# A delta-rule attention and an MLP on one core: work of the opening stage put in another order over ScalarE and VectorE

## The chip, the core and the metric

The kernel runs on one NeuronCore of a Trainium2 chip. The metric is the device time of one execution in microseconds (us); the time of a kernel is the median of its runs. The engines are TensorE (PE: matmuls and transposes, into PSUM), VectorE (DVE), ScalarE (ACT), GpSimd (POOL) and SyncE (SP, which issues nearly all loads). Each engine works off its own instructions in their order; a wait at the head of a queue holds everything behind it. Unless said otherwise, a time such as "at 43.6 us" is counted from the start of the profiled span.

## The reference

Two blocks run one after the other. The first is a delta-rule attention over 4 batches, 8 heads, 768 steps and head size 48; the second is an MLP over the 3072 rows of the first's output.

```python
k_n = k / (np.linalg.norm(k, axis=-1, keepdims=True) + 1e-06)
for t in range(S):                       # S = 768, state is (B, H, 48, 48)
    y[:, :, t] = einsum('bhd,bhde->bhe', q[:, :, t], state)
    v_old = einsum('bhde,bhd->bhe', state, k_n[:, :, t])
    state += b_t * einsum('bhd,bhe->bhde', k_n[:, :, t], v[:, :, t] - v_old)
x = y.transpose(0, 2, 1, 3).reshape(3072, 384)
h = x @ w_in                             # 384 x 2048
out = (0.5 * h * (1 + erf(h / sqrt(2)))) @ w_out      # 2048 x 384
```

The weights `w_in` and `w_out` come as 64-bit floats, which the kernel turns into 32-bit floats itself.

## The kernel before

**Tiles.** Time is cut into 12 chunks of 64 steps (`NC`). A chunk has two units (`NA`), each with two batches and 8 heads: 128 partitions are 2 batches x 64 steps. `tiles[c, a]` is unit `a` of chunk `c`; `first` are the four units of chunks 0 and 1, `zero` those of chunk 0, `one` of chunk 1, `third` of chunk 2, `fourth` of chunk 3. A unit's tiles are `Kp`, `Qp`, `V` (loaded), `Kt`, `Qt` (transposed), `P` (masked scores), `W`, `U` and `x`.

**A chunk's attention.** The recurrence within a chunk is a triangular system. Two chunks are a group, solved together: `grams` multiplies K with K, `flip` puts the 32 x 32 diagonal blocks into `Nu`, and 30 row steps on VectorE (`row_product`, L490, and `row_sum`, L495) invert them one row after another. `back` transposes the result into `XM` (L504) and `Zf` (L508). `join` (chunk pair 0, L529) or `join_run` (later pairs, L571) builds the off-diagonal block in two levels: TensorE's `psJ`, VectorE's product into `XM` (L540 or L583), `psJ` again, ScalarE's copy into `Zf` (L544 or L552). Then `against_state` (`psK`, L645), `subtract` (ScalarE copies `y`, L657, VectorE makes `W`, L658 and L659), `solve` (`psU`, L675, then copies to `U`, L680 and L682), `use` (`psY`, L694 and L703), `next_state` (L708), `read` (`x` out of `psY`, L716 for chunks 0 and 1, L718 later) and `turn` (transposes `psX`, then the copy to `xT`, L740).

For these a K row's length is needed. For chunks 2 and 3 `sum_of_squares` (L317, ScalarE, one head at a time) adds up squares, `prep` takes roots on GpSimd (`pow`, L332), `finish_both` makes the factors (L288 to L292), and `scale_head` (L355, ScalarE, one head at a time) multiplies V by the length; `scale_v` does so on GpSimd from chunk 4 on.

**The MLP.** For chunk `c`, `fc1(c, f)` makes hidden block `f` of 16 (six matmul records in `psH`, L763) and ScalarE's gelu writes it to `G` (L765). `psH` and `psO` share two PSUM buffers, so block `f` starts when the gelu of block `f - 2` is through. For chunks 0 and 1 `fc2` multiplies by `w_out` (`psO`, L776), with the copy to `o_sb` (L780) and two output DMAs issued by ScalarE (L770). From chunk 2 on the second product goes by Strassen's scheme with seven products (`second_layer`, L801, and VectorE's sums, L810 to L858); its weight sums need tiles that `late` makes room for, once the weights are decoded. `late` also makes the two `Kb` tiles, which must be cleared (L1007, ScalarE) before chunk 5's keys are loaded into them in blocks.

**The weights.** They come in 16 groups: 0 to 7 of `w_in` (two hidden blocks each), 8 to 15 of `w_out` (two `f` each). A group is decoded in five steps on VectorE, with one on ScalarE: `start_` (exponent bits, L218, then ScalarE's L223 into `w_e`), `upper` (L227), `lower` (L232), `sign` (L240, which needs L223) and `scaled` (L244, after which TensorE may use the group). Steps of group n + 1 stand between those of group n.

**What sets the order.** Up to the turn of chunk 0 all engines follow the order in which the code is written (`by_hand`, L907). After that a plan gives each step a due time: `on(first, last, steps)` spreads steps between two times on a scale where 57 to 115 is one chunk, `once` puts steps at one time, `at` counts in chunks. The steps are sorted by it; up to and including `late`, VectorE and ScalarE keep exactly that order, after it VectorE alone, and the scheduler orders the rest. `together` keeps the matmuls of its steps in one run on TensorE. Due times give an order, not a moment. `rows1` is the list of elimination steps of pair 1; `alternate(group(10, NW - 1), rows1[2:42])` mixes the decoding of the last groups with 40 of its row steps.

In the opening, ScalarE copies each `Qt` and `P` of chunks 0 and 1, and between units does four squares of chunk 2's K and four scalings of chunk 1's V:

```python
        queries([u])
        for h in range(4 * u.t, 4 * u.t + 4):
            sum_of_squares(tiles[2, h // H], h % H)
        for h in range(4 * u.t, 4 * u.t + 4):
            scale_head(tiles[1, h // H], h % H)
```

Of the kernel before, what the change touches and what calls it, by code (L numbers as in the profile page):

```python
# [16 lines left out]
def kernel(  # L17
# [28 lines left out]
    nc = tc.nc  # L46
    B, H, S, D = q.shape
# [91 lines left out]
    def load_v(c):  # L139
        if c >= NC:  # L140
            return
        for a in range(NA):
            u = tiles[c, a]
            u.V = io.tile([128, H, D], F32, tag="V", name="V", bufs=4)
            fetch_in(u.V, v, u)
# [162 lines left out]
    def sum_of_squares(u, h):  # L308

        if "both" not in ns:  # L310
            n23 = wk.tile([128, 2 * NA, H], F32, tag="n23", name="n23", bufs=1)
            ns[2], ns[3] = n23[:, 0:NA], n23[:, NA:]
            ns["both"] = n23
        if h == 0:
            u.ksq = wk.tile([128, H, D], F32, tag="ksq", name="ksq")
        kn = u.Kn if u.c == 2 else Qp[2 + u.a]
        nc.scalar.activation(u.ksq[:, h], kn[:, h, 0:D], ACT.Square,  # L317
                             accum_out=ns[u.c][:, u.a, h:h + 1])
# [593 lines left out]
    for n in range(2):  # L912
        fetch(n)
    load_k(2, "Kp")
    load_v(1)
    new_group(0)
    n0 = wk.tile([128, 2 * NA, H], F32, tag="n0", name="n0", bufs=1)
    for c in range(2):
# [21 lines left out]
    for u, ahead in zip(first, first[1:] + [None]):  # L940
        if ahead is not None:
            transposed(ahead, (1,))
        queries([u])
        for h in range(4 * u.t, 4 * u.t + 4):
            sum_of_squares(tiles[2, h // H], h % H)
        for h in range(4 * u.t, 4 * u.t + 4):
            scale_head(tiles[1, h // H], h % H)
    for a in range(NA):
        fetch_in(tiles[2, a].Qp[:, :, 0:D], q, tiles[2, a])
    for a in range(NA):  # L950
        fetch_in(Qp[2 + a][:, :, 0:D], k, tiles[3, a])
    for n in range(2, NS):
        fetch(n)
    for n in range(n_in, n_in + len(slots)):
        fetch(n)
    third = [tiles[2, a] for a in range(NA)]
# [22 lines left out]
    for step in (begin, exponents, upper, lower):  # L979
        for n in range(2):  # L980
            step(n)
    solve(first[:NA])
    sign(0)
    sign(1)
    use(first[:NA])
    for u in first[:NA]:
        read(u)
    scaled(0)
    scaled(1)
    for u in first[:NA]:  # L990
# [10 lines left out]
    def late():  # L1001
        start.close()
        more.append(ctx.enter_context(tc.tile_pool(name="late", bufs=1)))
        small[0] = ctx.enter_context(tc.tile_pool(name="few", bufs=1, space=bass.MemoryType.PSUM))
        for a in range(NA):
            Kb = more[0].tile([128, 2, NP, 2, HB], F32, name=f"Kb{a}")
            nc.scalar.mul(Kb.rearrange("q p j h n -> q (p j h n)"),  # L1007
                          low.rearrange("q a b -> q (a b)")[:, 0:NP * 4 * HB], 0.0)
            for c in range(5, NC, 2):
                tiles[c, a].Kb = Kb  # L1010

    def on(first, last, steps):

# [10 lines left out]
    def group(n, last=None):  # L1024
# [8 lines left out]
             once(79.2, (together, (solve, one))), once(83.2, (together, (use, one))),  # L1033
             once(85.2, *[(read, u) for u in one]), once(87.6, *[(next_state, u) for u in one]),
             once(87.7, *[(turn, u) for u in one])]
    plan += [on(57.8, 72.0, [(1.0, sum_of_squares, tiles[3, a], h)
                             for a in range(NA) for h in range(H)]),
             once(73.0, (load, 3), (prep, 2), (prep, 3))]
    plan += [on(54.3, 57.9, group(2)), on(57.9, 61.4, group(3)), on(61.4, 65.0, group(4)),
             on(67.5, 71.0, group(5)), on(71.0, 74.6, group(6)), on(76.8, 80.4, group(7)),  # L1040
             on(80.4, 84.0, group(8)), on(84.0, 87.5, group(9)),
             once(87.8, (finish_both,), *[s_[1:] for s_ in rows1[:2]]),
             on(91.9, 126.0, alternate(group(10, NW - 1), rows1[2:42])),
             on(126.1, 128.4, rows1[42:-3]), once(128.6, (late,))]
    for i in range(NF // 2):
        t = (84.2, 88.3)[i] if i < 2 else 92.1 + 5.68 * (i - 1)
        plan += [on(t, t + 2.5, [(1.0, fc2, u, 2 * i, 2 * i + 2) for u in zero])]
# [1 line left out]
        if i < EARLY // 2:  # L1049
# [6 lines left out]
    s2 = state_steps(2)  # L1056
    plan += [once(128.5, *[s_[1:] for s_ in rows1[-3:-1]]),
             once(131.6, (together, (against_state, third))), once(131.7, (subtract, third)),
             once(133.0, (together, join1[0])), once(133.1, rows1[-1][1:]),
             once(136.0, (together, join1[1]), (copy_out, "join", 4)),  # L1060
             once(138.0, (queries, third)), once(139.0, s2[1][1:]),
             once(140.0, (together, join1[2]), (copy_out, "join", 4)),
             once(143.0, s2[2][1:]), once(147.0, s2[3][1:], s2[4][1:]),
             once(141.0, (prep, 4)), once(150.0, (grams, [tiles[4, a] for a in range(NA)])),
             once(160.0, (finish, 4))]
    plan += [at(0.995, 1.0, [(1.0, load_v, 2)]), at(2.98, 2.981, [(1.0, sums_of_w)]), at(3.1, 3.11, [(1.0, last_sum_of_w)])]
    plan += [at(c - 0.4, c - 0.3, v_steps(c)) for c in range(4, NC)]
    plan += [at(c - 1.0, c - 0.99, [(1.0, load_v, c)]) for c in range(3, NC)]
    for c in range(4, NC):
        us = [tiles[c, a] for a in range(NA)]  # L1070
        t = {4: 1.8, 5: 2.25}.get(c, c - 2.9)
        plan += [at(t, t + 0.01, [(1.0, load_blocks, c, "Kb", k)])]
        t = 3.2 if c == 4 else c - (1.3 if c % 2 == 0 else 0.9)
        plan += [at(t, t + 0.01, [(1.0, load_blocks, c, "Qb", q)])]
        t = c - (2.1 if c % 2 == 0 else 2.4) if c > 5 else {4: 2.1, 5: 2.48}[c]
        plan += [at(t, t + 0.01, [(1.0, load_k, c, "Kn")])]
        plan += [at(c - 0.4, c - 0.39, [(1.0, load_k, c, "Kp")])]
        t = {4: 2.47, 5: 2.955}.get(c, c - (1.97 if c % 2 == 0 else 2.49))
        plan += [at(t, t + 0.01, [(1.0, turned_k, u) for u in us])]
        t = c + (0.05 if c % 2 == 0 else -0.34)  # L1080
        plan += [at(t, t + 0.01, [(1.0, turned_q, u) for u in us])]
# [9 lines left out]
    for w in range(3, NC):  # L1091
        two_ahead = w + 2 < NC
        if w % 2:
            if w == 3:
                plan += [at(w + 0.09, w + 0.092, [(1.0, transposed, u, (1,)) for u in fourth]
                            + [(1.0, together, *gram(5))])]
            plan += [at(w + 0.25, w + 0.95, state_steps(w, (), query(w)))]
            if two_ahead:
                rows = eliminate_steps(w // 2 + 1)
                plan += [at(w - (0.05 if w == 3 else 0.16), w - (0.04 if w == 3 else 0.15), [(1.0, prep, w + 2)]),  # L1100
                         at(w, w + 0.01, [(1.0, finish, w + 2)]),
                         at(w + 0.13, w + 0.18, rows[:2]), at(w + 0.18, w + 0.36, rows[2:26]),
                         at(w + 0.4, w + 1.06, rows[26:-3]), at(w + 1.07, w + 1.2, rows[-3:])]
        else:
            j0, j1, j2 = join_steps(w // 2)
            plan += [at(w + 0.23, w + 0.232, [(1.0, together, j0, *query(w))]),
                     at(w + 0.3, w + 0.301, [(1.0, together, j1, *gram(w + 2))]),
                     at(w + 0.35, w + 0.97, state_steps(w, (j2,), gram(w + 3)))]
            plan += spread("join", 2, w + 0.32, w + 0.355)
            plan += spread("join", 4, w + 0.455)  # L1110
            if two_ahead:
                plan += spread("gram", 1, w + 0.385, w + 0.42, w + 0.54, w + 0.58)
                plan += spread("gram", 1, w + 0.66, w + 0.661, w + 0.7, w + 0.701)
                plan += [at(w + 0.59, w + 0.591, [(1.0, prep, w + 2)]),
                         at(w + 0.9, w + 0.91, [(1.0, finish, w + 2)])]
# [36 lines left out]
```

## Time and profile before

| | |
|---|---|
| median of 5 runs | 662.63 us (660.55 to 662.95) |
| the profiled execution | 662.95 us, span 661.2 us |
| granted TensorE clock | 1.00 of full |
| TensorE busy | 633.7 us (96%) |
| VectorE busy | 441.2 us (67%) |
| ScalarE busy | 227.0 us (34%) |
| GpSimd busy | 78.6 us (12%) |
| first `psH` | at 59.3 us |

The page gives each engine's busy time, then the span in 40 slices of 16.5 us whose digits are busy tenths, then the chain of work that ended last, groups of instructions and DMA issues. In a row of the timeline the first number is the start, the second the time from the start of its first to the end of its last instruction, `x4` the number of instructions merged, and the bracket the idle time of that engine before it with what ended it. A row of waits gives the total, the number and the longest. Matmuls are counted in records, two for each f32 matmul of the code.

### The profile page before, as it was taken

What the parts mean: (1) busy time and instruction counts of PE and PEld (TensorE: products, weight loads), DVE (VectorE), ACT (ScalarE), POOL (GpSimd) and SP (SyncE); (2) the same over time, 40 slices, a digit from 0 to 9 for tenths busy, and PEclk for the clock granted to TensorE, in tenths of its full rate; (3) what the DMA queues carried; (4) which work ended last, traced back from release to release, by engine and by line L of the source; (5) the groups of instructions that cost most, each with busy time, mean ns of one, the idle gap of its engine ahead of it and who ended that gap; (6) DMA issues with size and microseconds to landing.
All of it is one profiled execution on the core that took longest, in us unless ns stands there. A gap on an engine that the chain in (4) does not pass through costs nothing.

```text
span 661.2 us, 20444 instructions
## 1 busy us (share of the span) xinstructions
PE 633.7 (96%) x8902; PEld 557.3 (84%) x8902; DVE 441.2 (67%) x920; ACT 227.0 (34%) x616; POOL 78.6 (12%) x79
## 2 busy tenths in 40 slices
PE   6678999899999999999999999999999999999997
PEld 5567887566789889989989989989989989989997
DVE  6969899995399855679755678755678744324022
ACT  3577754335441136132136132135132133131220
POOL 4050020003111011301011301011301010000000
PEclk9999999999999999999999999999999999999999
DMA  9875465033434233520233520212300210100101
GB/s 132 177 257 160 107 152 154 8 60 61 72 44 81 37 41 54 93 42 16 53 40 53 98 39 19 47 19 39 61 15 19 51 17 3 25 2 2 24 1 25
DMA packets 158426, 39.68 MB, mean 60 GB/s; under 512 B 150016, under 2 KB 153216, under 8 KB 158336
## 3 DMA queue, kind: packets, MB, share of 16 engines
q1 hardware_dynamic: 152464, 33.40, 26.5%
q10 hardware_dynamic: 5872, 4.97, 3.5%
q8 instruction: 70, 1.15, 0.8%
q14 instruction: 20, 0.16, 0.1%
HBM read 33.62 MB, written 4.72 MB: 58 GB/s over the span
## 4 chain that ended last, share of the span: by engine, by line
PE 77%; DVE 11%; ACT 3%; SPq 3%; DMA 3%; issue 1%; ACTq 1%; POOL 0%; DVEq 0%; POOLq 0%
PE psH L763 33%; PE psY L801 12%; PE psX L801 11%; PE psZ L801 4%; PE psG L395 3%; PE psK L645 3%; PE psO L776 3%; PE psJ L571 2%; SPq L96 2%; DVE Nu L495 2%; DVE tmp L490 2%; PE psY L694 2%; PE psU L675 2%; PE psY L703 1%; DMA Kp<-in_k_dram 1%
## 5 line engine op out<-in xcount | busy, mean ns | idle before, releaser
L763 PE MATMUL psH<-xT,w_in_sb 128*128 128x256 f32 x1152 | 260.9, 384 | 2.3 <-ACT G L765 1.1
L763 PEld LDWEIGHTS psH<-xT,w_in_sb 128*128 128x128 f32 x1152 | 217.7, 191 | 35.9 <-ACT G L765 2.5
L765 ACT ACTIVATE G<-psH 128x256 f32<-128x256 f32 x192 | 73.3, 384 | 188.5 <-PE psH L763 174.0
L490 DVE TENSOR_TENSOR tmp<-Nu 128x30 f32<-128x30 f32 (+9 forms) x180 | 62.3, 346 | 5.2
L495 DVE TENSOR_TENSOR Nu<-Nu,tmp 128x30 f32<-128x30 f32 (+9 forms) x180 | 60.6, 337 | 5.2
L801 PE MATMUL psY<-w_out_sb,G 128*128 128x192 f32 x304 | 54.2, 329 | 2.5 <-DVE u L844 1.4
L740 ACT COPY xT<-psX 128x384 f32<-128x384 f32 x24 | 11.5, 479 | 129.3 <-PE psX L739 126.4
L801 PE MATMUL psX<-w_out_sb,G 128*128 128x192 f32 x320 | 55.8, 328 | 0.0
L801 PEld LDWEIGHTS psY<-w_out_sb,G 128*128 128x128 f32 x304 | 49.1, 190 | 4.8 <-DVE u L847 3.2
L801 PEld LDWEIGHTS psX<-w_out_sb,G 128*128 128x128 f32 x320 | 52.4, 190 | 0.6
L332 POOL TENSOR_TENSOR n<-n,half 128x16 f32<-128x16 f32 x10 | 29.3, 2927 | 150.1 <-DVE n L306 117.5
L776 PE MATMUL psO<-w_out_sb,G 128*128 128x384 f32 x128 | 44.8, 493 | 2.2 <-DVE w_out_sb L244 2.2
L810 DVE TENSOR_TENSOR S<-G 128x512 f32<-128x512 f32 x20 | 13.8, 692 | 46.3 <-ACT G L765 45.8
L776 PEld LDWEIGHTS psO<-w_out_sb,G 128*128 128x128 f32 x128 | 23.3, 190 | 16.9 <-DVE w_out_sb L244 3.6
L658 DVE TENSOR_TENSOR W<-psK,V 128x384 f32<-128x384 f32 x22 | 12.2, 553 | 34.4 <-ACT y L657 34.4
L458 POOL MEMSET Zf<- 32x512 f32 x20 | 10.4, 519 | 178.7 <-DVE Zf L508 128.7
L815 DVE TENSOR_TENSOR G<-G 128x512 f32<-128x512 f32 x20 | 13.8, 693 | 25.0 <-PE psX L801 25.0
L801 PE MATMUL psY<-T,G 128*128 128x192 f32 x160 | 28.2, 329 | 0.0
L801 PE MATMUL psZ<-T,S 128*128 128x192 f32 x160 | 28.1, 329 | 0.0
L801 PE MATMUL psX<-T,G 128*128 128x192 f32 x160 | 28.1, 329 | 0.0
L801 PEld LDWEIGHTS psZ<-T,S 128*128 128x128 f32 x160 | 26.1, 190 | 0.3
L801 PEld LDWEIGHTS psX<-T,G 128*128 128x128 f32 x160 | 26.1, 190 | 0.2
(145 smaller groups left out, 851.7 us busy)
## 6 DMA issues: line engine op xcount, KB each, us to landing
Kp<-in_k_dram SPq DMA_DIRECT2D x76, 96.0 KB, 3.1
w_out_sb<-in_moe_w_in_dram SPq DMA_DIRECT2D x24, 256.0 KB, 4.3
V<-in_v_dram SPq DMA_DIRECT2D x48, 96.0 KB, 3.1
out_dram<-o_sb ACTq DMA_DIRECT2D x46, 96.0 KB, 2.2
w_raw<-in_moe_w_out_dram SPq DMA_DIRECT2D x10, 384.0 KB, 3.9
Zf<-in_moe_w_out_dram SPq DMA_DIRECT2D x6, 384.0 KB, 4.0
Qp<-in_q_dram SPq DMA_DIRECT2D x64, 32.0 KB, 2.1
Qp<-in_q_dram SPq DMA_DIRECT2D x16, 96.0 KB, 4.3
```

What stands on the lines that cost most here:

```text
L96: queues[p].dma_start(out=dst[HALF[p]], in_=src[2 * u.a + p, :, rows, :].rearrange("h t d -> t h d"))
L332: nc.gpsimd.tensor_tensor(flat, flat, half, op=ALU.pow)
L395: nc.tensor.matmul(psG[HALF[p], r, i * NP + j, :], lhsT=u.Kt[rows, p, j, :], rhs=(u.Qt if x else u.Kt)[rows, p, j, :], start=True, stop=True)
L490: nc.vector.tensor_tensor(tmp, nu[:, j + 1:, j:j + 1].to_broadcast([128, n, j]), nu[:, j:j + 1, 0:j].to_broadcast([128, n, j]), op=ALU.mult)
L495: nc.vector.tensor_tensor(nu[:, j + 1:, 0:j], nu[:, j + 1:, 0:j], tmps.pop(j), op=ALU.add)
L645: nc.tensor.matmul(u.psK[to, x, r, j, :], lhsT=(u.Qt if x else u.Kt)[rows, p, j, :], rhs=St[rows, u.a, p ^ r, j, :], start=True, stop=True)
L763: nc.tensor.matmul(psH, lhsT=w_in_sb[:, f // 2, m, f % 2 * 128:(f % 2 + 1) * 128], rhs=xTs[c][:, m, :], start=(m == 0), stop=(m == NM - 1))
L765: nc.scalar.activation(G[:, f, :], psH, ACT.Gelu)
L776: nc.tensor.matmul(u.psO, lhsT=G[:, f, u.a * 128:(u.a + 1) * 128], rhs=w_out_sb[:, f, :], start=(f == 0), stop=(f == NF - 1))
L801: nc.tensor.matmul(ps_, lhsT=lhs[:, f, :], rhs=rhs[:, f, :], start=first and f == 0, stop=f == FH - 1, skip_group_check=not first)
L810: nc.vector.tensor_tensor(W2["S"][:, fs], a21, a22, op=ALU.add)
L815: nc.vector.tensor_tensor(a12, a12, a11, op=ALU.subtract)
```

## The change

- In the opening, the 16 `scale_head` of chunk 1's V and the 16 `sum_of_squares` of chunk 2's K are no longer between the copies of the units. The scalings are due at 57.8 to 64.8, chunk 3's squares at 64.8 to 72.5 (57.8 to 72.0 before), chunk 2's squares at 73.1 to 79.0, and `prep` for both at 79.1 (73.0 before).
- The load of chunk 1's V is issued after the loads of chunk 2's Q, chunk 3's K and groups 2 and 3, instead of right after chunk 2's K.
- In chunk 0, `U` and `x` of unit 1 are copied out of PSUM by VectorE; ScalarE copied both units before.
- `finish_both` with the first two steps of pair 1 is due at 90.9 instead of 87.8. Thirty row steps instead of 40 stand between the steps of weight groups 10 to 15; the other ten come behind the last group.
- The joins, the queries and the state steps of chunk 2 are due 1.5 to 4 later on the plan's scale, and those of chunk 3 0.03 chunks later. The clearing of `Kb` is a step of its own, due at 147 instead of in `late` at 128.6, and the block load of chunk 5's keys is due at 2.6 chunks instead of 2.25.

```diff
@@ opening
     load_k(2, "Kp")
-    load_v(1)
...
         queries([u])
-        for h in range(4 * u.t, 4 * u.t + 4):
-            sum_of_squares(tiles[2, h // H], h % H)
-        for h in range(4 * u.t, 4 * u.t + 4):
-            scale_head(tiles[1, h // H], h % H)
...
     for n in range(2, NS):
         fetch(n)
+    load_v(1)
     for n in range(n_in, n_in + len(slots)):
         fetch(n)
...
-    solve(first[:NA])
+    solve(first[:NA], (nc.scalar.copy, nc.vector.tensor_copy))
...
-    for u in first[:NA]:
-        read(u)
+    for u, copy in zip(first[:NA], (nc.scalar.copy, nc.vector.tensor_copy)):
+        read(u, copy)
@@ late
-            nc.scalar.mul(Kb.rearrange("q p j h n -> q (p j h n)"),
-                          low.rearrange("q a b -> q (a b)")[:, 0:NP * 4 * HB], 0.0)
...
+    def clear_blocks():
+        for a in range(NA):
+            nc.scalar.mul(tiles[5, a].Kb.rearrange("q p j h n -> q (p j h n)"),
+                          low.rearrange("q a b -> q (a b)")[:, 0:NP * 4 * HB], 0.0)
@@ plan
-    plan += [on(57.8, 72.0, [(1.0, sum_of_squares, tiles[3, a], h)
+    plan += [on(57.8, 64.8, [(1.0, scale_head, tiles[1, a], h) for a in range(NA) for h in range(H)]),
+             on(64.8, 72.5, [(1.0, sum_of_squares, tiles[3, a], h)
                              for a in range(NA) for h in range(H)]),
-             once(73.0, (load, 3), (prep, 2), (prep, 3))]
+             once(73.0, (load, 3)),
+             on(73.1, 79.0, [(1.0, sum_of_squares, tiles[2, a], h)
+                             for a in range(NA) for h in range(H)]),
+             once(79.1, (prep, 2), (prep, 3))]
...
-             once(87.8, (finish_both,), *[s_[1:] for s_ in rows1[:2]]),
-             on(91.9, 126.0, alternate(group(10, NW - 1), rows1[2:42])),
-             on(126.1, 128.4, rows1[42:-3]), once(128.6, (late,))]
+             once(90.9, (finish_both,), *[s_[1:] for s_ in rows1[:2]]),
+             on(91.9, 126.0, alternate(group(10, NW - 1), rows1[2:32])),
+             on(126.1, 128.4, rows1[32:-3]), once(128.6, (late,))]
...
-             once(133.0, (together, join1[0])), once(133.1, rows1[-1][1:]),
-             once(136.0, (together, join1[1]), (copy_out, "join", 4)),
-             once(138.0, (queries, third)), once(139.0, s2[1][1:]),
-             once(140.0, (together, join1[2]), (copy_out, "join", 4)),
-             once(143.0, s2[2][1:]), once(147.0, s2[3][1:], s2[4][1:]),
-             once(141.0, (prep, 4)), once(150.0, (grams, [tiles[4, a] for a in range(NA)])),
+             once(136.0, (together, join1[0])), once(136.1, rows1[-1][1:]),
+             once(139.7, (together, join1[1]), (copy_out, "join", 4)),
+             once(142.0, (queries, third)), once(143.0, s2[1][1:]),
+             once(144.0, (together, join1[2]), (copy_out, "join", 4)),
+             once(146.5, s2[2][1:]), once(149.5, s2[3][1:], s2[4][1:]),
+             once(142.0, (prep, 4)), once(147.0, (clear_blocks,)), once(150.0, (grams, [tiles[4, a] for a in range(NA)])),
...
-        t = {4: 1.8, 5: 2.25}.get(c, c - 2.9)
+        t = {4: 1.8, 5: 2.6}.get(c, c - 2.9)
...
-            plan += [at(w + 0.25, w + 0.95, state_steps(w, (), query(w)))]
+            plan += [at(w + (0.28 if w == 3 else 0.25), w + (0.98 if w == 3 else 0.95), state_steps(w, (), query(w)))]
```

## Prediction

> **What bounds the kernel now.** First the page: who is busy where. Sections 1 and 2:
>
> ```profile
> PE 633.7 (96%) x8902; PEld 557.3 (84%) x8902; DVE 441.2 (67%) x920; ACT 227.0 (34%) x616; POOL 78.6 (12%) x79
> ...
> PE   6678999899999999999999999999999999999997
> ...
> DVE  6969899995399855679755678755678744324022
> ACT  3577754335441136132136132135132133131220
> ```
>
> TensorE is full from the fourth slice (59.3 us, the first `psH`) to the end, so a change is worth what it takes off before 59.3 us, plus the TensorE waits it removes after, less those it adds. TensorE's waits, all that are longer than 0.1 us between 59 and 240 us:
>
> ```profile
> PE psO L776 <- DVE w_out_sb L244: 2.2, 2, 1.1
> PE psY L801 <- DVE u L844: 1.4, 1, 1.4
> PE psH L763 <- ACT G L765: 1.1, 1, 1.1
> PE psH L763 <- ACT xT L740: 0.6, 1, 0.6
> PE psX L739 <- DVE x L718: 0.4, 1, 0.4
> ```
>
> Then the chain of waits in the head, in order of time:
>
> ```profile
> 28.50 1.01 ACT V L355 x4
> ...
> 36.42 0.90 ACT V L355 x4
> ...
> 45.08 1.92 PE psG L395 x64
> 46.99 1.02 PE psJ L529 x32
> 48.03 0.42 DVE XM L540
> ```
>
> From 28.5 to 48 us the chain is ScalarE's (scalings L355, squares L317, copies), then the TensorE work queued behind those copies. VectorE has its triangle ready long before, as the timeline shows, with two later waits that matter below:
>
> ```profile
> 41.59 1.97 DVE L508 STREAM_TRANSPOSE Zf<-Nu 128x1024 f32<-128x1024 f32 x1
> ...
> 48.03 1.75 DVE L540 TENSOR_TENSOR XM<-psJ,gm 32x256 f32<-32x256 f32 x4 [4.47 <-PE psJ L529]
> ...
> 82.10 0.56 DVE L658 TENSOR_TENSOR W<-psK,V 128x384 f32<-128x384 f32 x1 [0.80 <-ACT y L657]
> ```
>
> So 4.47 us of VectorE are lost at 43.6, and at 82.1 W waits for ScalarE's y (ended 81.97) though `psK` was complete at 80.6.
>
> **Step 1, the head: -4.47 us at L540.** Taken off ScalarE before 37.3 us: 16 scalings (4 x about 1.0 us), 16 squares (4 x 0.9 us), and the waits for K2 and V1 to land (1.95 and 1.40 us). ScalarE then follows TensorE's own pace, some 2.1 us a unit, so the last P copy is out near 29.5 instead of 35.5, G of chunk 2 near 34.2 instead of 40.9, and TensorE reaches `psJ` near 40.2 (6 us after G, as now). XM is transposed at 41.7 and that becomes the gate; `psJ`'s first half takes 1.0 us, and VectorE is back from Zf at 43.56, so L540 starts there: the wait goes whole. V1's four loads pass behind 14 others on SP's queue (Q2, K3, six weight loads): Q2 and K3 move up 5 us, V1 goes to about 38, and nobody reads it before 58. Cover for the loads: K2 lands at 26.1 as now, and is needed at 28.9.
>
> **Step 2, U and x: +2.9 us on VectorE, fc1 at 55.35 instead of 59.30.** Everything from L540 to ScalarE's exponents (51.77) moves 4.47 earlier: U of unit 0 is copied 49.1 to 50.1. Unit 1's copies now stand on VectorE, and in the built program they wait for ScalarE's last copy from the same `psU`, as W waits for y: 1.05 us idle, not parallel. Their cost isn't in the trace; the nearest rows are L680 on ScalarE (0.32) and L718 on VectorE with a second operand (0.27 to 0.36); I take 0.31, three for U and three for x, 1.85 in all (1.6 to 2.2). U1 at 51.05, `psY` 52.2, signs 51.05 to 52.8, x1 to 53.75, two `scaled` to 55.5; unit 1's transpose and xT, 1.5 us after x1 as now, end at 55.3. So TensorE starts 3.95 earlier, VectorE's group 2 (56.92) only 1.45 earlier.
>
> **Step 3, the first hidden blocks: 2.55 left.** VectorE no longer waits 0.71 for exponents behind xT (L240 at 60.11), so group 4's L218 ends at 61.6 instead of 63.75. ScalarE keeps that group's exponents ahead of gelu 1, which comes 1.07 later as now (63.78 to 64.85): 62.7. Hidden block f needs gelu f-2 (two PSUM buffers), so block 3 waits until 63.05 where TensorE would be there at 61.65: a new wait of 1.4. Blocks 3 on: 65.6 becomes 63.05.
>
> **Step 4, ScalarE to y: 2.45 lost again.** A scaling or a square costs ScalarE 0.23 back to back (0.90 and 0.91 for four). The scalings fit: ScalarE is through at 69.1 and block 6 ends at 70.6 (73.2 now). From gelu 6 to y its queue holds 18 squares where 7 stand now, 11 x 0.23 = 2.5, and there is no idle time to take them: in this stretch (73.25 to 81.53) ScalarE is busy for 8.15 of 8.28 us. So it becomes 10.8 us. y at 81.45, W at 82.05: as before. Behind it, gelu 10 comes at 82.6 and block 12 waits 2.3 us for it, which eats TensorE's lead too; `psY` of chunk 1 starts about 0.2 earlier than 89.89.
>
> [...] The trace: granted clock 1.00 in every window, yet the first 9 `psH` records fill 3.7 us (59 to 63), against 0.215 each later, so TensorE is slow at first; and after waits of 1.0 to 1.4 us (127, 131, 138, 219) the next group takes 2.85 as elsewhere. Whether 2.3 us makes it slow again no row shows: between 0 and 2.0 us (9 records at double time); I take 0, the longest wait that a row shows after 59 us being 1.37 and free. [...]
>
> **Step 5, 90 to 138 us: -3.45 us.** Ten row steps (j = 15 to 19) go behind the last decode; in the trace they take 0.31 to 0.44 each between weight steps, 3.5 us. The last L244 ends at 127.6 instead of 131.1, and TensorE's waits at 120.7 (0.2), 127.2 (1.03) and 131.2 (1.12) go. `late` no longer puts the clearing of Kb (1.15) behind the output DMAs on ScalarE; in the built program it stands ahead of the o_sb copies and waits only for that last L244 and landed loads, beside 2.85 us of `psO`. That is the 1.12 wait on gelu at 137.7, gone. Total now 0.2 + 2.35 + 1.12 = 3.65. `finish_both` needs two powers on GpSimd (3.0 each): the first can run from the end of chunk 3's squares (about 79), the second from 87.3 to 90.3, needed at 95.7: covered by 5 us, which it costs if the squares end that much later.
>
> **Step 6, chunk 2's joins: 1.2 given back.** VectorE's rows end no earlier (nothing removed, step 4 left it level). `psJ` level 1 needs L583, over at 146.25 in both. TensorE, 3.65 ahead, has eight more `psO` records (2.78) to put before it and waits 0.7. Those eight are then missing between `psY` and `psX`, which waits 0.8 for x instead of 0.37. Left: 3.65 - 0.75 - 0.45 = 2.45.
>
> **Step 7, chunk 3: -1.37.** Moved 0.03 later, its `psY` products stand before the outputs, and `u` (L844) before x on VectorE, so the wait at 218.9 has cover. Against: xT of unit 1 is then queued on ScalarE behind two output DMA issues (0.55 to 0.95 each); about 0.2 us of slack, so 0 to 0.8, and I take 0. Kb's loads for chunk 5 keep their place in SP's queue (from 128, needed at 177): free.
>
> **Sum.** 2.45 + 1.37 = 3.8. The profiled execution took 662.95 (span 661.2 and 1.75 around it): 659.15. It lies 0.32 above the median of the runs, so **658.8** for the median.
>
> **Rivals.**
> (a) VectorE's copies cost less: 0.25 each, and their wait for ScalarE is gone as the exponents end earlier than I put them. Then group 4's exponents, gelu 1, block 3, y and W all come 1.4 earlier: 657.4. For it: a copy has one operand where L718 has two. Against: W's wait for y shows such a wait kept to 0.13 us.
> (b) The head doesn't shorten: `psJ` still waits behind a late load (K2 kept ScalarE waiting 1.95, to 26.1). Then step 1's 4.47 is gone, all else stays: 663.2, no change. Against: K2's 2.8 us of cover.
> (c) Slower: ScalarE's queue is the bound from 62 to 90 us. If no operation overlaps the next, a square costs 0.24 + 0.19 (mean rows of L317), 0.20 more than I take: 18 of them put y 3.6 later, the 12 between y and U another 2.4, U at 93.3 instead of 87.2. `psY` is then 4.5 late; block 12 waits 5.9 us, and after waits of 3.4 us and more in the head TensorE is at half pace (64 `psG` in 1.99 us at 38.9, 1.16 at 180), another 2.0. Of that, step 5 pays back 3.45, the joins take 0.4, and step 7's cover goes: +3.5, 666.1. It decides from U copies at about 92 us on. For it: of 25 us from 62.2 to 87.2 ScalarE is busy 17.1 and gets 7.3 more. Against: the overlap of 0.2 stands in every run of four squares.
>
> **How the numbers follow.** What a measurement can tell is about 0.3%, 2 us: below 660.6 is faster, above 664.6 slower. My forecast 0.47 and (a) 0.15 are faster, 0.62; (b) and a half-lost head or the slow pace of step 4 alone, 0.17, same; (c) 0.21, slower. Range 656.2 to 665.2: at the low end (a) with step 6's 1.2 not given back, (b) inside, and the near part of (c). The forecast's own: 657.2 to 661.0, from the slow pace's 2.0 and step 7's 0.8 above, (a) below.
>
> **What would show it.** Right: L540 near 43.6 with no long wait; U by VectorE right after ScalarE's L682; the first `psH` near 55; TensorE waiting on gelu at block 3 and block 12; y near 81.5; no wait of `psO` on L244; a short wait of the level-1 `psJ`. Wrong: L540 still near 48 (b); group 4's exponents well before 61 (a); U copies of chunk 1 after 92 or `finish_both` waiting for GpSimd (c); `psH` records of 0.4 us after block 12 (clock).

## The result and the profile after

The changed kernel is neither faster nor slower: 661.87 us median (27 runs, 660.84 to 666.04) against 662.21 (48 runs), ratio of the runs 1.0004 with a 95% interval of 0.9995 to 1.0012. The forecast was 658.8. Its profiled execution took 663.8 us (span 662.1), 1.9 above its own median; that of before lay 0.7 above its median. So the two profiles stand 1.2 us further apart than the two medians do; the parts on the gap in `psU` and on the clock say what differs from run to run.

Sections 1 and 2 of the page after, the slices of TensorE, VectorE, ScalarE and of the granted clock:

```profile
PE   6948989998999999999999999999999999999997
...
DVE  6998898997399855678755678755678754324022
ACT  3544874425342136132136132136132133131220
...
PEclk9956989999999999999999999999999999999999
```

ScalarE is emptier in the third and fourth slice (33 to 66 us) and fuller in the fifth and sixth, as the change says. TensorE is as full as before. The clock reads half in the third slice, 0.6 in the fourth and 0.8 in the sixth, where the page before has 0.9 or more throughout. Only the sixth slice is new: in the head the kernel before was as slow (`psJ` takes 1.92 us in both), although its page doesn't show it (last section).

TensorE's waits in the whole trace after (who waits for whom: total, number, longest):

```profile
PE psJ L529 <- DVE XM L504: 5.0, 1, 5.0
PE psH L763 <- ACT G L765: 3.0, 2, 1.9
PE psU L675 <- issue: 2.2, 1, 2.2
...
PE psY L801 <- DVE u L847: 1.3, 1, 1.3
PE psJ L571 <- DVE XM L583: 1.3, 2, 0.7
PE psX L739 <- DVE x L718: 0.8, 1, 0.8
```

The waits of `psO` for L244 are gone, as forecast. The wait for `u` only changed its line (L844 to L847), and `psU` waits 2.2 us for "issue", which means for nothing that the profile shows.

Where the time stands at marks that both traces have (start of each, us):

| mark | before | after | difference | forecast |
|---|---|---|---|---|
| first L540 | 48.03 | 43.31 | -4.72 | -4.47 |
| first `psH` | 59.30 | 57.21 | -2.09 | -3.95 |
| hidden block 3 | 65.6 | 65.01 | -0.6 | -2.55 |
| `psK`, chunk 1 | 78.55 | 78.30 | -0.25 | -2.55 |
| `psY`, chunk 1 | 89.89 | 93.42 | +3.53 | -0.2 |
| `psK`, chunk 2 | 140.51 | 139.94 | -0.57 | -3.65 |
| `psG`, chunk 4 | 164.76 | 166.28 | +1.52 | -2.45 |
| span | 661.2 | 662.1 | +0.9 | -3.8 |

The head's gain arrives whole at L540, is gone at block 3, and turns into a loss of 3.5 us by 93 us. The later part then pays 4.1 back. The first L540 on VectorE, in the timelines of after and of e1 (an experiment below, whose head is that of the kernel before):

```profile
43.31 1.75 DVE L540 TENSOR_TENSOR XM<-psJ,gm 32x256 f32<-32x256 f32 x4
```

```profile
46.63 1.75 DVE L540 TENSOR_TENSOR XM<-psJ,gm 32x256 f32<-32x256 f32 x4 [3.34 <-PE psJ L529]
```

So the head of the kernel before varies by 1.4 us between two profiles (48.03 and 46.63), and the profile of before that the prediction worked from is the later one. In the ten other profiles that have the changed order without the moved masks, L540 starts at 43.25 to 44.20.

Two rows of TensorE before, `psU` and hidden blocks 10 to 13, both without a pause:

```profile
50.89 2.06 PE L675 MATMUL psU<-W,Zf 64*64 64x48 f32 x64
...
80.56 5.45 PE L763 MATMUL psH<-xT,w_in_sb 128*128 128x256 f32 x24
```

The rows of the losses, from the timeline of TensorE after:

```profile
46.16 0.78 PE L675 MATMUL psU<-W,Zf 64*64 64x48 f32 x15
49.10 1.54 PE L675 MATMUL psU<-W,Zf 64*64 64x48 f32 x49 [2.15 <-issue]
51.16 2.91 PE L694 MATMUL psY<-U,P 64*64 64x48 f32 x64 [0.53 <-ACT U L680]
...
65.01 4.15 PE L763 MATMUL psH<-xT,w_in_sb 128*128 128x256 f32 x18 [1.02 <-ACT G L765]
...
85.15 4.26 PE L763 MATMUL psH<-xT,w_in_sb 128*128 128x256 f32 x12 [1.95 <-ACT G L765]
```

`psU` stops after 15 of 64 records. Before block 12 TensorE waits 1.95 us for a gelu, and then blocks 12 and 13 take 4.26 us where twelve such records take 2.86 elsewhere. VectorE's rows after show the other half:

```profile
45.09 1.88 DVE L218 TENSOR_SCALAR w_e<-w_out_sb 128x768 uint32<-128x768 uint32 x2
...
51.73 0.36 DVE L680 COPY U<-psU 128x192 f32<-128x192 f32 x1 [2.08 <-ACT U L682]
...
84.09 0.56 DVE L658 TENSOR_TENSOR W<-psK,V 128x384 f32<-128x384 f32 x1 [3.09 <-ACT y L657]
```

The first weight step takes 1.88 instead of 1.03; VectorE stands idle 2.08 us for `U`; and `W` waits 3.09 us for `y` (0.80 before).

### The profile page after: what moved, and what is told of

The parts are those of the page before. It is cut to its first block, busy times and chain, and to the rows that moved or that the text cites. A ratio compares the mean times of both kernels' runs of the same rounds, so it can differ in the third digit from the quotient of the medians.

```text
span 662.1 us, 20440 instructions
## 1 busy us (share of the span) xinstructions
PE 632.1 (95%) x8902; PEld 556.3 (84%) x8902; DVE 443.9 (67%) x926; ACT 225.3 (34%) x610; POOL 82.2 (12%) x79
## 3 DMA queue, kind: packets, MB, share of 16 engines
q8 instruction: 70, 1.15, 0.8%
HBM read 33.62 MB, written 4.72 MB: 58 GB/s over the span
## 4 chain that ended last, share of the span: by engine, by line
PE 75%; DVE 18%; ACT 2%; issue 2%; DMA 2%; SPq 0%; POOL 0%; ACTq 0%; DVEq 0%; POOLq 0%
PE psH L763 31%; PE psY L801 11%; PE psX L801 11%; DVE tmp L490 4%; DVE Nu L495 4%; PE psZ L801 4%; PE psO L776 3%; PE psG L395 2%; PE psK L645 2%; PE psJ L571 2%; PE psU L675 2%; PE psY L694 2%; PE psY L703 1%; DVE w_e L240 1%; DVE T L787 1%
## 5 line engine op out<-in xcount | busy, mean ns | idle before, releaser
L801 PEld LDWEIGHTS psY<-w_out_sb,G 128*128 128x128 f32 x304 | 49.1, 190 | 4.4 <-DVE u L847 4.4
L332 POOL TENSOR_TENSOR n<-n,half 128x16 f32<-128x16 f32 x10 | 32.6, 3262 | 153.6 <-DVE n L306 112.5
L801 PEld LDWEIGHTS psY<-T,G 128*128 128x128 f32 x160 | 26.1, 190 | 0.2
```

Of the source, the lines that this page charges most:

```text
L332: nc.gpsimd.tensor_tensor(flat, flat, half, op=ALU.pow)
L801: nc.tensor.matmul(ps_, lhsT=lhs[:, f, :], rhs=rhs[:, f, :], start=first and f == 0, stop=f == FH - 1, skip_group_check=not first)
```

## The experiments

Each ran beside the kernel before on the same chip. The "ratio" is that to the kernel before, with its 95% interval. Each run has one profile; what is said of a row is said of that one execution. "Repairs" are edits of the changed kernel.

| run | what it is | median us | ratio |
|---|---|---|---|
| e1 | before + later part only | 660.08 | 0.9968 (0.9955 to 0.9982) |
| e2 | changed, `U` and `x` on ScalarE again | 660.79 | 0.9985 (0.9974 to 0.9997) |
| e3 | changed, chunk 2's squares in ScalarE's idle time | 660.67 | 0.9988 (0.9976 to 1.0000) |
| e4 | changed, TensorE kept busy in the head | 661.43 | 0.9989 (0.9977 to 1.0002) |
| e5 | changed, once more | 663.06 | 1.0015 (1.0002 to 1.0027) |
| e6 | changed, without the later part | 664.74 | 1.0047 (1.0032 to 1.0061) |
| e7 | e2 and e3 together | 659.03 | 0.9956 (0.9943 to 0.9969) |
| e8 | e7, six squares more, two masks earlier | 658.56 | 0.9955 (0.9939 to 0.9971) |
| e9 | e7, weight groups 8 to 10 loaded later | 657.40 | 0.9932 (0.9920 to 0.9944) |
| e10 | e7, six squares more | 657.26 | 0.9930 (0.9917 to 0.9943) |
| e11 | e9 and e10 together | 656.50 | 0.9915 (0.9903 to 0.9927) |
| e12 | changed, TensorE kept busy ahead of block 12 | 661.92 | 1.0000 (0.9991 to 1.0010) |

**The two halves of the change, e1 and e6.** e1 is the kernel before with the diff's lines from `finish_both` on; e6 is the changed kernel with those lines as before:

```diff
-             once(87.8, (finish_both,), *[s_[1:] for s_ in rows1[:2]]),
-             on(91.9, 126.0, alternate(group(10, NW - 1), rows1[2:42])),
+             once(90.9, (finish_both,), *[s_[1:] for s_ in rows1[:2]]),
+             on(91.9, 126.0, alternate(group(10, NW - 1), rows1[2:32])),
...
```

> The kernel before with only the part of the change that lies after 87 us: 30 row steps instead of 40 between the weight groups, finish_both later, the clearing of Kb as a step of its own, chunk 2's and 3's due times. By the prediction's steps 5 to 7 this is worth 3.45 + 0.2 - 1.2 + 1.37, so about 658.5 us. By the ledger of the trace after (psK of chunk 2 catches up 4.1 us, the joins give back 2.1, chunk 3 wins 0.6) it is worth 2.6: 659.6. If the row steps only move a wait to the joins, nothing: 662.2. Told apart by the time, and by where psK, psG of chunk 4 and the level-1 psJ stand.

> The changed kernel without its later part: 40 row steps, finish_both at 87.8, Kb cleared in late, chunk 2's and 3's due times as in the kernel before. The later part alone gained 0.32% (2.1 us). If the parts add up, the head is worth nothing by itself and this is level with the kernel before, 661.5 to 662.2. If the later part only pays back what the head's change loses (psY of chunk 1 was 3.5 us late in the profile after), this is 664 to 665. By the prediction's steps 1 to 4 it is 0.2 faster than before.

e1 gained 0.32%, 2.1 us: nearer to what the table of marks gives for the stretch behind `psY` of chunk 1 (4.1 - 2.1 + 0.6 = 2.6) than to the forecast's 3.8. e6 lost 0.47%, 3.1 us. The sum, +1.0, is about what the whole change does (0.3 to 1.0 by its two series). So the head's half, meant to be the main gain, is a loss, and the later half only pays it back. TensorE's waits between 59 and 170 us in e1:

```profile
PE psJ L571 <- DVE XM L583: 1.3, 2, 0.7
PE psX L739 <- DVE x L718: 0.8, 1, 0.8
```

From `psK` of chunk 2 to `psG` of chunk 4 it takes 26.33 us in e1 and 26.34 after, 24.25 before: the joins cost 2.1 with or without the head's changes.

**VectorE's copies, e2.**

```diff
-    solve(first[:NA], (nc.scalar.copy, nc.vector.tensor_copy))
+    solve(first[:NA])
...
-    for u, copy in zip(first[:NA], (nc.scalar.copy, nc.vector.tensor_copy)):
-        read(u, copy)
+    for u in first[:NA]:
+        read(u)
```

> The changed kernel with U and x of chunk 0's second unit copied by ScalarE again, as before. If VectorE's copies and its wait for U are what lost the head's gain: VectorE begins group 2 near 53.5 instead of 57.46, fc1 starts 5.7 us after ScalarE's first U copy as in the kernel before (56.4 instead of 57.2), block 3 has no wait, psK of chunk 1 comes near 76.5 instead of 78.3, and the time is about 660. If ScalarE's queue from gelu 6 to y alone sets the later part, the head's order doesn't matter: 661.9, block 12 waits as now. If the copies on VectorE were a gain (the prediction's view of fc1): 663.

The first theory was right in its direction and short in its sizes: VectorE began group 2 at 53.18 (53.5 expected), fc1 came at 55.21 (56.4), and `psK` at 74.48 (76.5), 3.8 us earlier than after; but block 3 still waited 0.44, and the time is 660.79 where 660 was expected. Some of that is chance: `psU`'s gap was 0.79 here. The lead then went the same way as after, here in the rows of TensorE from block 3 on:

```profile
61.18 4.15 PE L763 MATMUL psH<-xT,w_in_sb 128*128 128x256 f32 x18 [0.44 <-ACT G L765]
...
81.33 4.54 PE L763 MATMUL psH<-xT,w_in_sb 128*128 128x256 f32 x12 [1.95 <-ACT G L765]
```

The wait of 1.95 is there again although all stands 3.8 us earlier: it hangs on ScalarE's queue, not on when chunk 0 began. The slow records behind it are there too.

**The squares, e3, and both repairs, e7.** In e3 the 16 squares go to where ScalarE idles after (37.8 to 43.3 us); e7 has e2's edit as well:

```diff
     grams(fourth)
+    for a in range(NA):
+        for h in range(H):
+            sum_of_squares(tiles[2, a], h)
     for fn, *args in rows:
...
-             once(73.0, (load, 3)),
-             on(73.1, 79.0, [(1.0, sum_of_squares, tiles[2, a], h)
-                             for a in range(NA) for h in range(H)]),
-             once(79.1, (prep, 2), (prep, 3))]
+             once(73.0, (load, 3), (prep, 2), (prep, 3))]
```

> The changed kernel with chunk 2's 16 squares on ScalarE right behind the copies of chunk 3's gram, where ScalarE is idle for 5.5 us (37.8 to 43.3), and the roots due at 73.0 as before. If the squares ahead of y are the cause (y 2.1 late, block 12 waits 1.95, 12 records at half pace cost 1.4): y near 81.3, W without a wait, no wait at block 12, TensorE at full pace there, psY of chunk 1 near 90.0 instead of 93.4, and 658.5 us if the joins let 3.4 through, 660 if they take half. If ScalarE's total work or the head sets psY: 661.9, with block 12 waiting as now. [...]

> The changed kernel with both single repairs: U and x of the second unit on ScalarE, and chunk 2's squares in ScalarE's idle 5.5 us. If they remove two different losses (VectorE's late weight groups, ScalarE's late y and the slow pace behind it), psK of chunk 1 is near 74.5, y comes without the eleven squares, block 12 waits at most 0.6, psY of chunk 1 is near 87.2 instead of 93.4 and the time is 2.4 below that of the first repair: 658.4. If they remove the same loss: 660.7, psY near 89.7.

In e3 block 12's wait fell to 0.61, its records were back at 2.86 for twelve, and `psY` came at 91.03 instead of 93.42; `y` was at 82.67 instead of the expected 81.3, since 14 of chunk 3's squares still stand between gelu 6 and `y` (they were spread from 57.8 before, and are from 64.8 now). In e7 `psY` came at 88.05 and the time fell by 0.44%: the repairs remove two different losses and add up. `psK` was at 75.36, not 74.5, with a `psU` gap of 1.88.

**More squares, e10, and the masks, e8.** e10 moves six of chunk 3's squares into the same idle time; e8 also puts the masks of chunk 1's scores right behind their products:

```diff
+    for h in range(6):
+        sum_of_squares(tiles[3, 0], h)
...
         queries([u])
+        if u.c == 1:          # e8 only
+            masked(u)
```

> The kernel with both repairs, and two steps more: six of chunk 3's squares also in ScalarE's idle time of the head, and GpSimd's masks of chunk 1's scores right behind their products, beside VectorE's row steps, instead of at 43.6 to 46.1. If VectorE's first L218 pair takes 1.88 instead of 1.03 because it starts beside a mask, it is back at 1.03 and every group is 0.85 earlier; y comes 1.4 earlier still than with both repairs, block 12 doesn't wait, and the time is 1 us below theirs: 657.4. If masks beside the row steps slow these (0.2 to 0.4 us each at present), XM comes late and the time is 1 us above theirs.

> The kernel with both repairs, and six of chunk 3's squares too in ScalarE's idle time of the head (without the moved masks). Six squares less ahead of y are 1.35 us: W's wait for y falls from 2.19 to about 0.8, block 12's wait of 0.61 goes, psY of chunk 1 is 0.6 to 1.0 earlier than 88.05, 658.2. If y is not the gate any more: 659.0. Beside the kernel with moved masks it also tells what those cost: there XM came 2.4 us later, since two row steps took 1.37 instead of 0.41 beside a mask, and one L218 pair got 0.85 back.

e10: `W`'s wait 1.14, no wait at block 12, `psY` at 86.64, 657.26. It also had the luck of a short `psU` gap (0.52). e8 shows what GpSimd's masks do to VectorE, in the timeline of VectorE:

```profile
27.23 0.41 DVE L490 TENSOR_TENSOR tmp<-Nu 128x238 f32<-128x238 f32 x1
27.68 1.37 DVE L495 TENSOR_TENSOR Nu<-Nu,tmp 128x238 f32<-128x238 f32 x1
29.08 1.37 DVE L490 TENSOR_TENSOR tmp<-Nu 128x240 f32<-128x240 f32 x1
...
47.59 1.03 DVE L218 TENSOR_SCALAR w_e<-w_out_sb 128x768 uint32<-128x768 uint32 x2
```

Beside each of the two masks (27.39 to 30.18 on GpSimd, 1.4 each) one row step takes 1.37 instead of 0.41, 1.92 us more for both; in return L218 is back at 1.03. So the 0.85 that L218 lost after (45.09 to 46.97) goes with the last mask, which ended at 46.09. The masks must stand somewhere, and beside the row steps they cost VectorE more (1.92) than beside L218 (0.85).

**The gap in `psU`, e5, e4 and e9.** e5 is the changed kernel once more. e4 adds matmuls that nobody reads where TensorE idles. e9 is e7 with three loads issued later:

```diff
+    transposed(fourth[0], (0,))
+    keep_busy(4)              # e4: 4 matmuls of 128x256 into a free PSUM tile
+    transposed(fourth[1], (0,))
     grams(fourth)
+    keep_busy(10)
@@ e9
     load_v(1)
-    for n in range(n_in, n_in + len(slots)):
-        fetch(n)
...
     scaled(0)
     scaled(1)
+    for n in range(n_in, n_in + len(slots)):
+        fetch(n)
```

> The changed kernel once more, for a second profile beside the kernels of this series. If the 2.15 us for which psU waited on nothing that the profile shows is a chance of code loading, it differs here (0.8 in the kernel with U and x on ScalarE, 2.07 in the one with the squares moved, none in the one with extra matmuls), and with it fc1 (57.2) and the time; if it belongs to the order of the instructions, it is 2.1 again. Time about 661.9 either way.

> The changed kernel with 14 extra 128x256 matmuls on TensorE whose result nobody reads: 4 between the transposes of chunk 3's K (idle 32.1 to 34.2) and 10 behind chunk 3's gram (idle 36.6 to 41.6). If the granted clock follows how much of a stretch TensorE is busy, it stays at 1.00 through 35 to 43: psJ takes 1.2 instead of 1.9, and if it holds on, psY 1.2 instead of 2.9 and the first 18 psH 3.9 instead of 6.8; psJ starts at 41.6 as now. Then fc1 comes about 2 us earlier and the time is near 660, since block 3 still waits for VectorE's groups. If the clock falls all the same, the ten take 8 us instead of 4.3, psJ starts 2 to 3 us late and the time is 664. If TensorE's pace in the head is hidden by VectorE's: 661.9.

> The kernel with both repairs (659.0 us), and the loads of weight groups 8 to 10 issued behind the decoding of groups 0 and 1 instead of ahead of it: about 2.3 MB less on the DMA engines before 46 us. If psU's gap of 1.9 to 2.1 us is TensorE's next block of code standing behind these loads (its 16 KB packet came at 46.3, and psU went on 2.4 us after it, as in five other profiles), the packet comes 2 us or more earlier, the gap is gone, U comes 2 us earlier, fc1 starts near 54.2 instead of 56.1, and psK of chunk 1 comes 0.9 earlier, as in the kernel with a gap of 0.8 (74.5): 658.1. If the packet's time is set by TensorE's own progress, the gap stays and so does the time, 659.0. If groups 8 to 10 come late, 660 or more.

In e5 the gap was 2.04 us, and the time 0.15% above the kernel before (the first series had 0.04%; the intervals overlap). A 16 KB packet of queue 8, which the DMA view calls instruction (70 packets, 1.15 MB in all), was on its way at 46.65 after, and TensorE went on 2.45 us later. In the seven other profiles with a gap (e2, e3, e5, e6, e7, e10, e12) the packet came between 45.5 and 47.5 and the gap ended 2.3 to 2.5 us after it. In e8, with the same loads, it came at 46.09 and `psU` ran through: its sixteenth record, about 49.1, was due 3.0 us after the packet. In e9 the packet came at 42.7, and `psU` runs through. That TensorE's own progress sets the packet's time, the rival in e9's expectation, doesn't fit: the packet came when TensorE had begun 1486 instructions (matmuls and weight loads) in the profile of before and 1519 in e9, but 1633 to 1728 in the eight with a gap. Here e9's `psU`, then two stretches each of the windows view, of e9 and of after (the last two numbers are the DMA engines' busy share and GB/s):

```profile
46.24 2.06 PE L675 MATMUL psU<-W,Zf 64*64 64x48 f32 x64
```

```profile
40.00:44.00 4.00, 1.92 (x64) 1.81 (x64) 3.96 (x4) 2.84 (x21) 4.00 (x5) 0.50 0.03 6
44.00:48.00 4.00, 3.60 (x127) 3.57 (x128) 3.92 (x8) 2.94 (x8) 4.00 (x3) 0.50 0.02 4
```

```profile
40.00:44.00 4.00, 1.92 (x64) 1.81 (x64) 3.96 (x4) 0.66 (x2) 4.00 (x5) 0.50 0.98 365
44.00:48.00 4.00, 2.62 (x79) 2.44 (x80) 3.92 (x8) 2.98 (x7) 2.09 (x2) 0.50 0.46 181
```

In e9 the DMA engines are nearly empty here (0.03) and the packet came at 42.7; after they are at 0.98 from 40 to 44 us, the packet came at 46.65, and `psU` stood for 2.15 us. e9 is 1.6 us faster than e7. That `psU` waits for the packet, and the packet for the weight loads, is the author's reading of these times; the profile names no cause, and before, the packet came at 42.7 too with the engines at 1.02 (42 to 46 us).

e4 is the clearest test of the prediction's steps 2 and 3, by accident: a packet came at 38.55, and it had no gap. Its rows:

```profile
55.35 6.61 PE L763 MATMUL psH<-xT,w_in_sb 128*128 128x256 f32 x18 [0.57 <-ACT xT L740]
63.15 4.15 PE L763 MATMUL psH<-xT,w_in_sb 128*128 128x256 f32 x18 [1.18 <-ACT G L765]
...
83.29 4.54 PE L763 MATMUL psH<-xT,w_in_sb 128*128 128x256 f32 x12 [1.95 <-ACT G L765]
```

fc1 at 55.35 and block 3 at 63.15 are the forecast's 55.35 and 63.05. As for its own question: the clock did stay at 1.00 up to 46 us and `psJ` took 1.20 and 1.49 instead of 1.92, but was at half again by the first `psH` (0.84 from 44 to 48 us, 0.50 from 59 to 60); the time of 661.43 doesn't settle what that is worth. It does tell that the gap alone is not the miss: with the first block and block 3 where the forecast had them, e4 is still 2.6 us above the forecast, and 1.7 of that is in its last row (4.54 instead of 2.86).

**The clock at block 12, e12.**

```diff
-            fc1s(0, 10, 4, 74.9, 79.1), ...
+            fc1s(0, 10, 2, 74.9, 77.0), once(77.05, (together, (keep_busy,), (fc1, 0, 12))),
+            fc1s(0, 13, 1, 78.05, 79.1), ...
```

> The changed kernel with three extra matmuls of 128x256 (6 records, 1.3 us), whose result nobody reads, between hidden blocks 11 and 12, where TensorE waits 1.95 us for the gelu. They end before block 12 may start, so nothing moves but the clock. If the wait is what lowers the granted clock 1.3 us after its end (12 records in 4.26 instead of 2.86, psU in 1.36 instead of 1.15), the clock stays at 1.00 there and the time falls by up to 1.6, by about half of that on average, since one profile of two showed the wait without the drop: 661 to 661.5 where the changed kernel has 661.9 to 663.1. If the drop has another cause, it is there again.

```profile
81.77 1.46 PE L1029 MATMUL psW<-P,ident 128*128 128x256 f32 x6
83.88 2.86 PE L763 MATMUL psH<-xT,w_in_sb 128*128 128x256 f32 x12 [0.65 <-ACT G L765]
```

The wait, cut to 0.65 us by the extra matmuls, leaves the clock alone. The time (661.92) can't be told from the changed kernel's, so the drop's price in the median stays open; in a single profile it is 1.4 to 1.7. The clocks of the single executions point the same way: of the changed kernel's in both series, the twelve with a mean granted clock of 0.981 or more took 660.84 to 662.76 us, and the eleven at 0.977 took 662.88 to 666.04 (the other seventeen, at 0.966 to 0.979, took 661.25 to 663.94). That is a link and not a price, since a longer stretch at half pace in the head lowers the mean as well. When the clock changed, the windows view after tells in slices of 1 us (clock third from the end):

```profile
85.00:86.00 1.00, 0.85 (x4) 0.78 (x5) 0.97 (x3) 1.00 (x9) 0.72 (x1) 1.00 0.72 122
86.00:87.00 1.00, 1.00 (x5) 0.84 (x4) 1.00 (x3) 0.68 (x6) 0.00 (x0) 0.72 0.42 46
87.00:88.00 1.00, 1.00 (x4) 0.76 (x3) 1.00 (x2) 1.00 (x4) 0.00 (x0) 0.50 0.49 61
...
89.00:90.00 1.00, 1.00 (x29) 0.67 (x32) 1.00 (x2) 0.56 (x3) 0.00 (x0) 0.57 0.72 139
```

Full slices read 1.00 or 0.50 here; as a mix of these two, 0.72 is 44% at full. So the clock falls at 86.44, 1.3 us after TensorE is back at work, and rises at 89.86. Read the same way it falls at 35.24 (0.62 from 35 to 36) and rises at 62.56 (0.72 from 62 to 63). These four times are 8, 7 and 1 steps of 3.41 us apart: they lie on a grid. So do those of e2 (58.02, 81.92, 85.34), e4 (60.38, 84.26, 87.68) and e6 (63.36, 87.24, 90.66), each 7 steps and 1 apart. After, the wait of 83.20 to 85.15 lies inside one step (83.03 to 86.44). In e2, e4 and e6 too it lies inside one, and the clock fell at that step's end, to 0.02 us. In e12, seven steps behind its rise at 60.17, a boundary would lie at 84.06 and the step before it begin at 80.65, so the uncut wait (81.93 to 83.88) would have lain inside it, as those four did. In e5 a boundary at 84.92, seven steps behind its rise at 61.02, cuts the same wait (83.60 to 85.55) in two, and block 12 runs at full pace:

```profile
85.55 2.86 PE L763 MATMUL psH<-xT,w_in_sb 128*128 128x256 f32 x12 [1.95 <-ACT G L765]
```

**The version that beats both, e11.** e9's and e10's edits together.

> Both repairs, six squares more in ScalarE's idle time, and the loads of groups 8 to 10 issued later: the version that the runs so far point to. If the parts add up: 657.3, ratio to the kernel before 0.993. If TensorE then waits for VectorE's fourth group (block 3) for what it gains before: 658.2.

```profile
75.66 5.70 PE L763 MATMUL psH<-xT,w_in_sb 128*128 128x256 f32 x24
...
82.67 2.83 PE L763 MATMUL psH<-xT,w_in_sb 128*128 128x256 f32 x12 [0.23 <-DVE w_in_sb L244]
85.43 0.68 PE L694 MATMUL psY<-U,P 64*64 64x48 f32 x32
```

656.50 us, 0.85% faster than the kernel before, and 0.8 below what was expected. Blocks 10 to 13 run without a wait, and `psY` of chunk 1 starts at 85.43, 8 us earlier than after.

## Why the prediction was wrong

The chain of reasons held in most of its links. Two steps failed: step 2, which had no term for a gap in `psU` (0 taken, 2.15 measured), and step 4, which took the slow pace behind a wait at 0 (1.6 measured). Steps 6 and 7 were smaller misses.

**Step 1 (head) was right.** L540 at 43.31 (43.56 forecast), no wait at it. But the 4.47 was read from one profile; by e1's it would have been 3.34, so part of the forecast gain was chance in the head of before. It left ScalarE idle for 5.53 us, which the prediction did not name, and which became the place for the squares.

**Step 2 was right in its own working, and failed on something that it did not have: the gap in `psU`.** Without the gap (e4) fc1 is at 55.35, with it at 57.21. That e4 meets the forecast to the hundredth is luck: there L218 took 0.79 more than taken, the six copies 0.32 more, and the 1.05 that VectorE was to wait for ScalarE's last copy fell to nothing. The gap is the mis-sized term: 0 taken, 2.15 in the trace after, 0.6 in e12 with the same head. What may have announced it in the trace of before: "issue" waits of 1.4 and 0.8 in the head, and the DMA engines at 0.93 to 1.02 from 34 to 46 us. There the instruction packet came at 42.7 and `psU` began at 50.89; after, `psU` began 4.7 us earlier, at 46.16, and the packet came at 46.65, behind its start. In e9, with three groups of weights loaded later, it came at 42.7 again, ahead of `psU` (46.24), and there was no gap. What VectorE's copies cost was near (2.17 for six where 1.85 was taken), and their wait for L682 grew to 2.08 behind the gap. The choice itself may still be bad: e2, without the copies, is 0.15% faster than before where the changed kernel is level, but part of that can be its shorter gap.

**Step 3** follows: block 3 at 65.01 for 63.05. In e4 it is 63.15.

**Step 4 had the wait right and the pace behind it wrong.** Gelu 6 to `y` took 10.63 for 10.8, block 12 waited 1.95 for 2.3, and a square cost 0.22 where 0.23 was taken. Slow pace after the wait was taken at 0, with 2.0 as the other end; it was 1.4 for the twelve `psH` and 0.2 for `psU`. The prediction had named this sign (slow `psH` records after block 12). What failed was to carry a free wait of 1.37, the longest in the trace of before, over to 2.3: a wait of 1.95, 57% of one step of 3.41, was enough in the four profiles in which it lay inside one. With the lead of 2.55 already lost in step 3, wait and pace went straight into `psY`: +3.53.

**Step 5 was right, and a little more:** 4.1 gained between `psY` of chunk 1 and `psK` of chunk 2, for 3.45. All named waits went. The cover of `finish_both` shrank from 5 us to 1.2: the second root started at 90.13 instead of 87.3, took 6.50 on GpSimd where 3.0 was taken (3.13 in e5; why is open) and ended at 96.63; L288 came at 97.82.

**Step 6** gave back 2.1 for 1.2: `psJ` waits twice (1.3) instead of once (0.7), and `psX` 0.8. VectorE's rows are the gate, as it said, with L504 at 142.39 (138.55 before). In e1, where `psY` of chunk 1 is not late, it is 2.1 too, so this miss is not a follow-up of the head's; no run takes it apart further.

**Step 7** gained 0.6 for 1.37: the wait for `u` moved one instruction on (L847, 1.3), so `psY`'s products did not cover the chain of VectorE's sums. No run tests this step by itself.

**The rivals.** (b) did not happen. (a) did not either. (c) had the right stretch, ScalarE's queue from 62 to 90 us, the slow pace of 2.0 and a late `psY` (+4.5 forecast, +3.5 measured), but the wrong reason, squares at 0.43 each; U came at 90.78, short of its point of 92, and step 5 repaid it. The sum of what was missed, from the table of marks: 3.7 by `psY`, 0.9 in the joins, 0.75 in chunk 3, less 0.65 in step 5, 4.7 in all, which is the difference of the two profiles (+0.9) from the forecast (-3.8). The medians miss the forecast by 3.1 only: the profiled execution had a long gap and the fall of the clock, which not every execution has.

## What to carry to other kernels

Work taken off the path in the head must go where the engine then idles, not to the next stretch in which that engine is full: the same 16 squares cost 1 to 2 us at 73 us (e3 beside the changed kernel, e7 beside e2), and at 38 they moved neither L540 (43.44) nor the first `psH` (57.25). When a change pulls an engine's work forward, ask also what becomes of its instruction packets and of the clock: bulk loads that are needed late can stand behind that work (with three groups loaded later, `psU`'s gap of 1.88 us in e7 was gone in e9), and waits that come near 2 us can be filled (1.41 us inside one clock step stayed free in e12, 1.94 in e6 did not).

## What the runs showed of the hardware

- TensorE's clock changed on a grid of 3.41 us (after at 35.24, 62.56, 86.44 and 89.86) that does not start with the kernel. Behind waits of 1.94 and 1.95 us inside one step it fell to 0.50 at the step's end in four profiles of four (after, e2, e4, e6); behind waits of 1.98 and 1.95 across a boundary it stayed at 1.00 (e5, at 63.43 and 83.60), and so it did behind one of 1.57 with 1.41 inside a step (e12, from 62.17) and one of 0.65 (e12). Where the grid lies differs from run to run of one kernel (a rise at 62.56 after, at 61.02 in e5), and so does the gap in `psU` (0.57 to 2.15 us in the same instruction order up to there).
- In the kernel before, the small matmuls (32x32 and 64x48 tiles) kept TensorE almost without a pause from 46.9 to 52.95 us, with records still slow (`psJ` 1.92, 1.20 later). The granted clock reads 1.00 there, and in the whole of that trace. After, it reads 1.00 all the way to its first change at 35.24, beside 64 `psG` in 1.99 us (25.76) as beside 64 in 1.16 (29.94), so a reading of 1.00 ahead of the first change did not tell the pace. In e1, with the same head, it is on record: half from 44.31 to 61.38. One whole step of the grid there, in the windows view, with TensorE busy throughout and no rise at its end:

```profile
47.72:51.14 3.42, 3.42 (x124) 3.36 (x125) 3.38 (x7) 2.51 (x6) 1.31 (x1) 0.50 0.02 5
```

Whether the small tiles are the reason is not shown.
- `psU` stood idle up to 2.15 us and went on 2.45 us after a 16 KB instruction packet (after, 46.65), behind a stretch with the DMA engines at 0.98 (40 to 44 us); with them at 0.03 (e9) the packet came at 42.7, with no gap.
- Beside a GpSimd mask of 1.4 us a VectorE row step took 1.37 us instead of 0.41 (e8, twice).
